# Attention, two MoE layers, one core: another order for the work and the loads of the first two token blocks

## Chip, cores, metric

One core of one Trainium2 chip runs the whole kernel. The metric is the device time of one execution in microseconds (us), as the median of several executions.

## What is computed

The reference, cut to its arithmetic (B = 4 batches, H = 8 heads, S = 576 positions, D = 64; then 2304 tokens of width 512):

```python
def _attn_ref(q, k, v, g_norm):
    kv = np.einsum('bhsd,bhse->bhde', k, v)
    out = np.einsum('bhsd,bhde->bhse', q, kv)
    rms = np.sqrt(np.mean(out * out, axis=-1, keepdims=True) + 1e-06)
    return (out / rms * g_norm)

def _moe_ref(x, w1, w2, w3, w_out):          # w1, w2, w3: 512 x 768, w_out: 768 x 512
    h = np.maximum(np.maximum(x @ w1, x @ w2), x @ w3)
    return (h @ w_out)

def _moe2_ref(x, domain_probs, w1, w2):      # 4 experts, 512 x 1024 and 1024 x 512
    p = domain_probs / (domain_probs.sum(-1, keepdims=True) + 1e-09)
    for e in range(E):
        out += p[:, e:e + 1] * (np.maximum(x @ w1[e], 0.0) @ w2[e])
```

The weights of the first MoE layer arrive as float64. The kernel takes each as a 128 x 512 piece of 64-bit words and makes float32 of it with integer operations.

## The kernel before

The 2304 tokens are worked on in six blocks of 384. The kernel first computes the attention of all tokens, mixed with the first MoE layer for blocks 0 and 1, then the first MoE layer for blocks 2 to 5, then the second MoE layer. Everything is recorded in one hand-made order: each engine runs its instructions in the order in which the program text issues them, and all loads go through the one queue of SyncE (SP in the profile). Matrix products that need precision take each operand as a rounded part ("hi") and a rest ("lo") and add three products.

The change touches the first stretch only, that is attention plus the first MoE layer of blocks 0 and 1. Two strings of tokens set its order.

The string `order` (L634) is the order of the loads. `k` loads one half of a batch's k and v (four DMAs, together 1.18 MB; half 0 serves heads 0 to 3), `q` loads one group of 256 query positions (512 KB; `q2` is the tail group, in four DMAs), `w` loads one weight piece (512 KB). `pump` (L639) issues from the head of this list as far as buffers allow: six for q, three pairs for k and v, three for weight pieces. It is called once at the start and after each step. Behind its first call stand the two small loads of `g_norm` (L660) and the VectorE instruction that doubles `g` (L661).

The string `steps` (L678) is the order of the work. A dot and letters behind a step name the engines of its copies: a is ACT, v is DVE, p is POOL.

- `Kbc` (att_kv): 20 matmuls of 64 columns for two heads of batch b. The fourth of a batch copies the result from the PSUM bank into the tile kvb by four copies.
- `Ti` (att_T): eight transposes of query group i and two copies into the tile qT.
- `Oi` (att_O): 16 matmuls of qT with kvb, two squares on ACT, two sums and one scale-and-add on DVE. `Ni` (att_N): the norm, one ACT and four small DVE operations, then two multiplications on DVE.
- `Xi` (att_X): eight transposes back and two copies into yT. `Sj` (split_x): the hi and lo parts of block j (128 x 1536).
- `Aijf` (moe1_a): product i of block j for the feature group f, 12 matmuls, followed by a copy or a maximum. `Hjf`: hi and lo of the hidden values. `Pf` (moe1_o): block 0 times the w_out piece f, 12 matmuls.
- `a` and `b`: the conversion of weights, by position. Each `a` (conv_a, L217) starts three things for three successive weights: the split into hi and lo of the oldest one (split_h on the engine named first, split_l on POOL where the second letter is p), conv0 of the newest (an ACT operation and a minimum on POOL, L197 and L198), and it leaves conv1 of the middle one (three DVE operations, L205, L206, L209), and a lo part on DVE, for the next `b`.

The converted weights lie in 24 places (w_buf), so none of them is reused in this stretch. PSUM banks are taken in turn: three for transposes and A products, four for O and P, one for K.

Of the kernel before, what the change touches and what calls it, by code (L numbers as in the profile page):

```python
# [21 lines left out]
def tile_attn_moe_moe2(  # L22
# [23 lines left out]
    nc = tc.nc  # L46
# [8 lines left out]
    T = 384  # L55
# [7 lines left out]
    def f32(ap):  # L63
        return ap.bitcast(F32)
# [94 lines left out]
    worder = [("a", 0, 0)]  # L159
    for f in range(NF):  # L160
        worder += [("a", 1, f), ("a", 2, f)] + [("a", 0, f + 1)] * (f + 1 < NF) + [("o", 0, f)]
    N1 = 4 * NF
# [16 lines left out]
    def split_h(w, t, eng="a"):  # L179
        copy(eng, w[:, 0, :], t)  # L180

    def split_l(eng, w, t, key):
        eng.tensor_tensor(out=w[:, 1, :], in0=t, in1=f32(w[:, 0, :]), op=ALU.subtract)  # L183
        wt[key] = w

    def new_w(key):
        return w_buf[worder.index(key)]
# [4 lines left out]
    conv = {}  # L192
# [18 lines left out]
        )  # L211

    cpos = [0, 0, 0, 0]

    def conv_a(pool, eng="ap"):  # L217

        rest = []
        if cpos[3] < cpos[2]:  # L220
            key = worder[cpos[3]]
            w, t = new_w(key), conv.pop(key)
            split_h(w, t, eng[0])
            cpos[3] += 1
            if eng[1] == "p":
                split_l(nc.gpsimd, w, t, key)
            else:
                rest.append(lambda: split_l(nc.vector, w, t, key))
        if cpos[2] < cpos[1]:
            key1 = worder[cpos[2]]  # L230
            rest.insert(0, lambda: conv1(pool, key1))
        if cpos[1] < cpos[0]:
            conv0(pool, worder[cpos[1]])
            cpos[1] += 1
        return rest

    def load_w_to(pool, n):
        while cpos[0] < min(n, N1):
# [379 lines left out]
    with tc.manual_schedule():  # L618
        cv_cm = tc.tile_pool(name="cvp", bufs=3, reuse_waits="tile")
        cvp = cv_cm.__enter__()  # L620
# [9 lines left out]
        for t in kvb:  # L630
# [1 line left out]


        order = (  # L634
            "k00 q0 k01 q1 q2 k10 k11 q3 q4 q6 k20 q5 k21 k30 k31 w w w q8 q9 w"
        ).split()
        free = {"q": 6, "k": 3}

# [28 lines left out]
        def new_acc(n):  # L667
            return [bank("acc") for c in range(n)]
# [7 lines left out]


        steps = (  # L678
# [8 lines left out]
        ).split()  # L687
        for st in steps:
            st, *en = st.split(".")
            kind, at = st[0], [int(x) for x in st[1:]]  # L690
            if kind == "T":
                att_T(xq, *at, *en)
                free["q"] += 1
            elif kind == "K":
                att_kv(kvb, *at, *en)
                free["k"] += at[1] % 2
            elif kind == "O":
                att_O(xq, kvb, *at)
                if at[0] == len(groups) - 1:
                    att_cm.__exit__(None, None, None)  # L700
                    wp = ctx.enter_context(tc.tile_pool(name="wp", bufs=1, side="right", reuse_waits="tile"))
                    wr.append(wp.tile([P, 16 * 2 * DM], F32R, name="wr"))
                    w_buf.extend(part(wr[0], n * 2 * DM, 2 * DM, 2) for n in range(16))
            elif kind == "X":
                att_X(*at, *en)
                if at[0] == len(groups) - 1:
                    xq_cm.__exit__(None, None, None)
                    hs_cm = tc.tile_pool(name="hs", bufs=NF, side="right", reuse_waits="tile")
                    hs = hs_cm.__enter__()
            elif kind == "N":  # L710
                att_N(*at)
            elif kind == "A":
                i, j, f = at
                moe1_a(i, j, f, xs[j], *en)
            elif kind == "H":
                j, f = at
                hidden[j, f] = moe1_split(hs if j else None, j, f, *en)
            elif kind == "P":
                acc = acc or new_acc(KD)
                moe1_o(*at, hidden.pop((0, *at)), acc)  # L720
            elif kind == "S":
                xs.append(split_x(*at, *en))
            elif kind == "a":
                rest = conv_a(cvp, *en)
            elif kind == "b":
                for fn in rest:
                    fn()
            pump()
        assert cpos[3] == N1
        cv_cm.__exit__(None, None, None)  # L730
        moe1_store(0, acc)
        xs = xs[2]
# [54 lines left out]
        for e in range(E):  # L787
            for pr in range(NPR):
                n = (e * NSB - 1) * NPR + pr
# [11 lines left out]
        for n, (e, sb, pr) in enumerate(rounds):  # L801
            last_sb = sb == NSB - 1
            more = not (e == E - 1 and last_sb)
            rest = iter(())
            if before is not None:
                e0, sb0, pr0 = before
                rest = second(n - 1, pr0)
# [60 lines left out]
```

## Time and profile before

| | |
|---|---|
| median of 3 executions | 1148.13 us (1147.34 to 1148.51) |
| the profiled execution | 1146.83 us, its span 1145.0 us |
| PE (TensorE matmul) | 1120.5 us busy, 98% of the span |
| PEld (TensorE weight load) | 1031.7 us |
| DVE (VectorE) | 562.7 us, 49% |
| ACT (ScalarE) | 390.9 us, 34% |
| POOL (GpSimd) | 236.8 us, 21% |
| chain that ended last | PE 88%, DVE 5%, DMA 2%, SPq 2%, ACT 1% |

The page cuts the span into 40 slices of 28.6 us. In tenths (9 is 90% or more), PE's busy share is 6 in the first slice, 9 in the next three, 8 in the fifth, and 9 in all others but the last (8). DVE shows 1, 8, 8, 9, 8, 6 in the first six slices and 2 to 7 later. The DMA row shows 9, 9, 3, 4, 4, 1 in the first six. So the first stretch is where something other than PE can decide. Busy time of an engine that nobody waits for costs nothing; the rows further below are therefore mainly waits and starts.

### The profile page before, as it was taken

Reading aid. Unit: us, or ns where it says so; the run is one execution under the profiler, and the core shown is the slowest. Engines: PE = TensorE matmul, PEld = TensorE weight load, DVE = VectorE, ACT = ScalarE, POOL = GpSimd, SP = SyncE. Lnnn points to the kernel's source line nnn. Section 1 sums busy time; section 2 is a strip of 40 time slices with the busy share of each in tenths; the row PEclk is TensorE's granted clock in tenths of the full one; section 3 lists DMA queues with packets and bytes.
Section 4 is the critical chain, followed back from the end, with each engine's and each line's share of the span. In section 5 each row is a group of like instructions: output and inputs, shape, how many; then the busy total and the mean of one; then the engine's idle time right before and its main releaser. Section 6 shows DMA issues by size and latency. Waiting matters only on the chain.

```text
span 1145.0 us, 15032 instructions
## 1 busy us (share of the span) xinstructions
PE 1120.5 (98%) x6096; PEld 1031.7 (90%) x6096; DVE 562.7 (49%) x842; ACT 390.9 (34%) x699; POOL 236.8 (21%) x178
## 2 busy tenths in 40 slices
PE   6999899999999999999999999999999999999998
PEld 5888899999999888889888988888888888888887
DVE  1889862222325544344754436573535576343523
ACT  3653321121113434253634233452424253332321
POOL 1356740000401320205220202412020522011000
PEclk9999999999999999999999999999999999999999
DMA  9934410000201402014140403332030625040111
GB/s 255 283 107 130 147 47 29 1 28 1 65 29 37 157 1 102 9 56 138 60 171 1 165 1 131 127 122 99 29 138 9 212 65 193 1 153 14 48 63 56
DMA packets 77990, 99.59 MB, mean 87 GB/s; under 512 B 10336, under 2 KB 53344, under 8 KB 77920
## 3 DMA queue, kind: packets, MB, share of 16 engines
q1 hardware_dynamic: 77920, 98.62, 27.0%
q8 instruction: 48, 0.79, 0.3%
q14 instruction: 22, 0.18, 0.0%
HBM read 75.01 MB, written 23.59 MB: 86 GB/s over the span
## 4 chain that ended last, share of the span: by engine, by line
PE 88%; DVE 5%; DMA 2%; SPq 2%; ACT 1%; issue 1%; POOL 1%; DVEq 0%; ACTq 0%
PE bank L575 35%; PE bank L535 30%; PE bank L247 15%; PE bank L413 6%; DMA v<-in_v_dram 1%; DVE cv_a L206 1%; DVE cv_a L209 1%; PE bank L269 1%; DMA k<-in_k_dram 1%; PE bank L362 1%; DVE cv_a L205 1%; SPq L154 0%; PE bank L319 0%; DVE fa L392 0%; SPq L135 0%
## 5 line engine op out<-in xcount | busy, mean ns | idle before, releaser
L575 PE MATMUL bank<-wr,hr 128*128 128x512 f32 x792 | 227.0, 395 | 0.0
L559 DVE TENSOR_TENSOR fa<-bank,fa 128x384 f32<-128x384 f32 x144 | 80.1, 557 | 212.5 <-ACT fa L556 119.2
L575 PEld LDWEIGHTS bank<-wr,hr 128*128 128x128 f32 x792 | 147.0, 188 | 20.7
L517 POOL TENSOR_TENSOR fa<-fa 128x768 f32<-128x768 f32 x48 | 97.3, 2037 | 300.2 <-DMA fa<-y_d 243.0
L247 PE MATMUL bank<-xr,wr 128*128 128x384 f32 x792 | 145.2, 340 | 5.6 <-DVE fa L392 2.2
L247 PEld LDWEIGHTS bank<-xr,wr 128*128 128x128 f32 x792 | 139.6, 188 | 8.4 <-DVE fa L392 3.2
L486 POOL TENSOR_TENSOR w1s<-w1s 128x256 f32<-128x256 f32 x64 | 53.9, 862 | 421.8 <-DMA w1s<-in_moe_w_dram 374.7
L556 ACT ACTIVATE fa<-bank 128x384 f32<-128x384 f32 x144 | 70.6, 490 | 194.3 <-PE bank L535 194.3
L535 PE MATMUL bank<-rb,wr 128*128 128x384 f32 x648 | 131.5, 338 | 0.3 <-DVE hr L543 0.3
L535 PE MATMUL bank<-xr,wr 128*128 128x384 f32 x648 | 131.6, 338 | 0.0
L535 PEld LDWEIGHTS bank<-rb,wr 128*128 128x128 f32 x648 | 116.6, 188 | 10.2 <-DVE hr L543 0.6
L535 PEld LDWEIGHTS bank<-xr,wr 128*128 128x128 f32 x648 | 116.7, 188 | 9.6
L575 PE MATMUL bank<-wr,xr 128*128 128x512 f32 x324 | 100.8, 396 | 0.0
L392 DVE TENSOR_TENSOR fa<-bank,fa 128x384 f32<-128x384 f32 x72 | 39.8, 555 | 117.7 <-PE bank L247 117.5
L247 PE MATMUL bank<-xr,wl 128*128 128x384 f32 x504 | 90.5, 335 | 0.0
L247 PEld LDWEIGHTS bank<-xr,wl 128*128 128x128 f32 x504 | 87.4, 188 | 0.2 <-DVE wl L183 0.2
L575 PE MATMUL bank<-wl,hr 128*128 128x512 f32 x288 | 86.3, 394 | 0.0
L543 DVE SCALAR_TENSOR_TENSOR hr<-fa,hr 128x384 fp32r<-128x384 f32 x72 | 50.0, 695 | 42.6 <-ACT hr L542 42.6
L575 PEld LDWEIGHTS bank<-wr,xr 128*128 128x128 f32 x324 | 60.7, 188 | 10.8
L542 ACT ACTIVATE hr<-fa 128x384 fp32r<-128x384 f32 x72 | 37.8, 525 | 77.4 <-DVE fa L559 77.4
L575 PEld LDWEIGHTS bank<-wl,hr 128*128 128x128 f32 x288 | 53.4, 188 | 6.9
L542 ACT ACTIVATE xr<-fa 128x384 fp32r<-128x384 f32 x48 | 25.2, 525 | 96.7 <-DVE fa L559 96.7
(132 smaller groups left out, 1477.5 us busy)
## 6 DMA issues: line engine op xcount, KB each, us to landing
fa<-y_d SPq DMA_DIRECT2D x22, 768.0 KB, 6.2
stage_a<-in_moe_w_dram SPq DMA_DIRECT2D x18, 512.0 KB, 3.4
o_d<-fa SPq DMA_DIRECT2D x36, 256.0 KB, 3.7
fa<-o_d SPq DMA_DIRECT2D x36, 256.0 KB, 5.3
w1s<-in_moe_w_dram SPq DMA_DIRECT2D x32, 256.0 KB, 3.1
w2s<-in_moe_w_dram SPq DMA_DIRECT2D x32, 256.0 KB, 4.0
y_d<-fa SPq DMA_DIRECT2D x6, 768.0 KB, 3.8
o_d<-ob SPq DMA_DIRECT2D x18, 256.0 KB, 2.0
```

What stands on the lines that cost most here:

```text
L205: nc.vector.tensor_scalar(out=ti, in0=ti, scalar1=3, scalar2=None, op0=ALU.logical_shift_left)
L247: nc.tensor.matmul(ps, w[:, wi, c * P : (c + 1) * P], x[xi][:, c, :], start=(n == 0), stop=(n == 3 * KD - 1),)
L392: nc.vector.tensor_tensor(out=ms[j, f], in0=ps[:, :T], in1=ms[j, f], op=ALU.max)
L413: nc.tensor.matmul(acc[c][:, :T], w[:, wi, c * P : (c + 1) * P], h[hi], start=(f == 0 and n == 0), stop=(f == NF - 1 and n == 2),)
L486: eng.tensor_tensor(out=st[:, o], in0=st[:, a], in1=st[:, b], op=ALU.subtract)
L517: eng.tensor_tensor(out=yb[:, o], in0=yb[:, a], in1=yb[:, b], op=op)
L535: nc.tensor.matmul(out, w[wi][:, c * P : (c + 1) * P], y[yi][:, c, :], start=(i == 0 and k in BEGIN), stop=(i == 5), skip_group_check=k no ...
L542: nc.scalar.activation(out=h[0], in_=src, func=AF.Relu)
L543: nc.vector.scalar_tensor_tensor(out=h[1], in0=src, scalar=0.0, in1=f32(h[0]), op0=ALU.max, op1=ALU.subtract)
L556: nc.scalar.activation(out=s[k // 2], in_=a, func=AF.Copy)
L559: nc.vector.tensor_tensor(out=t, in0=x, in1=t, op=ALU.add)
L575: nc.tensor.matmul(banks[i], h[a, i // TPB][hi][:, i % TPB * P : (i % TPB + 1) * P], w[a][wi], start=(pr == 0 and a == 0 and m == 0), stop ...
```

## The change

The helper that converted by position is gone. Each stage of each weight is now a step of its own: `cN` is conv0 of weight N, `dN` conv1, `sN` its split with the engines named behind the dot. The two strings are new. No arithmetic is added or removed; the last two stretches of the program are as before.

```diff
-    cpos = [0, 0, 0, 0]
-    def conv_a(pool, eng="ap"):
...
+    cpos = [0, 0, 0]
+    def conv2(key, eng="ap"):
+        w, t = new_w(key), conv.pop(key)
+        split_h(w, t, eng[0])
+        split_l(nc.gpsimd if eng[1] == "p" else nc.vector, w, t, key)
...
-            "k00 q0 k01 q1 q2 k10 k11 q3 q4 q6 k20 q5 k21 k30 k31 w w w q8 q9 w"
+            "q1 q0 k00 k01 w q2 k10 k11 q3 w q4 k20 k21 q6 q5 k30 k31 w w q8 q9"
...
-            "K00 T0 K01 K02 K03 T1 O0 O1 K10 a N0 T2.av b K11 a N1 K12 K13 T3.av O2 b X0 N2 O3 T4 X1 "
-            "a.vp b O4 N3 K20 T5 a b a.vv K21 K22 N4 K23 X2 S0.pp X3 S1.vp O5 T6 b N5 K30 X4.va a.pp O6 "
-            "K31 b a.av X5 b K32 K33 N6 T8 a O7 b T9 O8 A000 a X6 b N7 A010 a.vp b A100 a.vp O9 b X7 "
...
+            "K00 K01 T1.av T0 K02 K03.avav c0 O1 O0 N1 K10 N0 T2 K11 d0 X1 K12 K13.vvaa T3.av X0.vv O3 T4.va "
+            "N3 c1 O2 K20 s0.pp O4 K21 N2 X3 K22 N4 T6 K23 d1 S0.pp X2 T5.av O6 S1.pp O5 N6 N5 X4 K30 K31 c2 "
+            "K32 c3 K33 d2 d3 s1.pp s2.pp A000 T8 X6 O8 O7 A200 s3.pp N8 c4 c5 A010 T9 d4 d5 X5 O9 A110 A100 "
...
```

Three places show how the instructions move. The first is the head of DVE's queue. Before, behind the doubling of g stand the sums of O0 and O1 (ss) and the first norm (rr); kvb_124 below is the tile of batch 0, bank_73 the bank of the K steps.

```order
L661 TENSOR_SCALAR g_75<-g_75 128x1
L333 TENSOR_REDUCE ss_253<-xt_244 128x8 x2
L334 TENSOR_SCALAR a_254<-ss_253 128x16
L333 TENSOR_REDUCE ss_269<-xt_260 128x8 x2
L334 TENSOR_SCALAR a_270<-ss_269 128x16
```

The same place of DVE's queue in the changed kernel:

```order
L645 TENSOR_SCALAR g_75<-g_75 128x1
L70 COPY qT_192<-bank_71 128x512
L70 COPY kvb_124<-bank_73 64x4x64 x2
L317 TENSOR_REDUCE ss_256<-xt_247 128x8 x2
L318 TENSOR_SCALAR a_257<-ss_256 128x16
```

One copy of T1 (qT_192) and two of K03 (kvb_124), which were ACT's, now stand on DVE between the doubling of g and the first sums.

The second place is the head of the queue of loads on SP. Before:

```order
L153 DMA k_0_128<-in_k_dram 128x4x256
L154 DMA k_0_128<-in_k_dram 64x4x64
L153 DMA v_0_131<-in_v_dram 128x4x256
L154 DMA v_0_131<-in_v_dram 64x4x64
L139 DMA q_134<-in_q_dram 128x8x128
```

And in the changed kernel, from its first load to the g load (the k01 pair and the rest of k10 left out):

```order
L139 DMA q_128<-in_q_dram 128x8x128
L139 DMA q_130<-in_q_dram 128x8x128
L153 DMA k_0_132<-in_k_dram 128x4x256
L154 DMA k_0_132<-in_k_dram 64x4x64
L153 DMA v_0_135<-in_v_dram 128x4x256
L154 DMA v_0_135<-in_v_dram 64x4x64
...
L176 DMA stage_a_0_144<-in_moe_w_dram 128x4x128
L135 DMA q_146<-in_q_dram 32x8x128 x4
L153 DMA k_0_151<-in_k_dram 128x4x256
...
L644 DMA g_75<-in_g_norm_dram 64x1 x2
```

Two query groups now stand ahead of the first k and v, and a weight piece (stage_a) ahead of the g load.

The third place is DVE's queue around the step T5, whose tile is qT_478 before and qT_583 after. Before, both its copies are on ACT, behind a norm's square root:

```order
L342 ACTIVATE s_459<-ss_415,eps 128x16
L68 ACTIVATE qT_478<-bank_72 128x512
L68 ACTIVATE qT_478<-bank_70 128x512
L342 ACTIVATE s_525<-ss_452,eps 128x16
L68 ACTIVATE kvb_124<-bank_73 64x4x64 x4
```

In the changed kernel this is DVE's queue from the end of N2 over N4 and d1 (cv_a) to T5's second copy:

```order
L337 TENSOR_TENSOR xt_443<-bank_68,rr_510 128x512
L327 RECIPROCAL rr_538<-s_537 128x16
L328 TENSOR_TENSOR rr_538<-a_479,rr_538 128x16
L329 TENSOR_TENSOR rr_538<-rr_538,s_537 128x16
L330 RECIPROCAL rr_538<-rr_538 128x16
L337 TENSOR_TENSOR xt_469<-bank_69,rr_538 128x4x2x64
L337 TENSOR_TENSOR xt_469<-bank_66,rr_538 128x4x2x64
L205 TENSOR_SCALAR cv_a_0_440<-cv_a_0_440 128x512
L206 SCALAR_TENSOR_TENSOR cv_a_0_440<-stage_a_0_188,cv_a_0_440 128x512
L209 SCALAR_TENSOR_TENSOR cv_a_0_440<-stage_a_0_188,cv_a_0_440 128x512
L70 COPY qT_583<-bank_72 128x512
```

T5's second copy now stands on DVE behind a norm and a conversion.

## Rows read from the trace of the kernel before

**Rows 1.** Stretches: busy PE, PEld, DVE, ACT, POOL; clock; DMA share; GB/s
```profile
0.00:57.80 57.80, 45.80 (x532) 40.91 (x532) 28.37 (x63) 28.69 (x57) 15.09 (x15) 0.97 1.10 269
57.80:100.00 42.20, 40.50 (x266) 38.75 (x265) 38.58 (x71) 22.13 (x43) 25.53 (x18) 1.00 0.34 110
100.00:128.00 28.00, 23.06 (x123) 20.82 (x122) 27.28 (x38) 9.27 (x17) 20.51 (x15) 1.00 0.44 138
128.00:165.70 37.70, 37.67 (x213) 37.34 (x213) 30.13 (x45) 11.53 (x20) 24.64 (x20) 1.00 0.23 77
165.70:1145.00 979.30, 973.43 (x4970) 893.84 (x4968) 438.33 (x629) 319.29 (x564) 151.02 (x112) 1.00 0.22 74
```

**Rows 2.** Groups by line, PE, 57.9 to 128 us: busy, mean | idle before
```profile
L247 PE MATMUL bank<-xr,wr 128*128 128x384 f32 x101 | 19.7, 346 | 4.9 <-DVE fa L392 1.6 <-ACT fa L68 1.5 <-ACT wr L68 1.0
...
L295 PE MATMUL bank<-ident,q 128*128 128x128 f32 x16 | 2.2, 278 | 1.2 <-DMA q<-in_q_dram 1.2
```

**Rows 3.** Timeline of PE, start: start us, us, what [idle before]
```profile
7.56 1.53 PE L269 MATMUL bank<-v,k 128*64 128x64 f32 x20 [7.56 <-DMA v<-in_v_dram]
9.59 1.94 PE L295 MATMUL bank<-ident,q 128*128 128x128 f32 x8 [0.49 <-DMA q<-in_q_dram]
...
18.09 4.97 PE L319 MATMUL bank<-kvb,qT 128*128 128x128 f32 x32
```

**Rows 4.** Rate of the DMA engines, 5 to 56 us
```profile
DMA packets 21486, 14.32 MB, mean 281 GB/s; under 512 B 4687, under 2 KB 21481, under 8 KB 21481
```

**Rows 5.** The load of g (timeline of SP; its tile) and DVE's first instruction
```profile
16.57 1.19 SPq L660 DMA_DIRECT2D g<-in_g_norm_dram  x2
...
DMA to landing us min/median/max: 6.2/6.4/6.5
...
23.78 0.15 DVE L661 TENSOR_SCALAR g<-g 128x1 f32<-128x1 f32 x1 [23.78 <-ACT xt L332]
```

**Rows 6.** Timeline of ACT and DVE: the copies of kvb and qT
```profile
16.52 1.56 ACT L68 ACTIVATE kvb<-bank 64x256 f32<-64x256 f32 x4 [4.36 <-PE bank L269]
...
28.89 0.68 DVE L70 COPY qT<-bank 128x512 f32<-128x512 f32 x1
```

**Rows 7.** Timeline of PE, 42 to 58 us: a wait, then steps at full clock
```profile
42.94 1.88 PE L269 MATMUL bank<-v,k 128*64 128x64 f32 x40 [1.81 <-DMA v<-in_v_dram]
...
49.45 1.04 PE L295 MATMUL bank<-ident,q 128*128 128x128 f32 x8
50.41 0.95 PE L269 MATMUL bank<-v,k 128*64 128x64 f32 x20
...
52.22 1.95 PE L319 MATMUL bank<-kvb,qT 128*128 128x128 f32 x16
54.10 0.95 PE L269 MATMUL bank<-v,k 128*64 128x64 f32 x20
54.98 1.09 PE L362 MATMUL bank<-ident,xt 128*128 128x128 f32 x8
56.00 1.82 PE L269 MATMUL bank<-v,k 128*64 128x64 f32 x40
```

**Rows 8.** Stretches around the changes of PE's pace, columns as in Rows 1
```profile
18.20:20.60 2.40, 2.40 (x13) 2.40 (x13) 0.00 (x0) 1.54 (x3) 1.04 (x1) 1.00 1.12 290
21.00:23.00 2.00, 2.00 (x20) 1.88 (x18) 0.00 (x0) 1.20 (x2) 0.00 (x0) 1.00 1.14 283
44.60:47.90 3.30, 3.30 (x19) 3.18 (x18) 1.90 (x6) 2.97 (x7) 0.00 (x0) 0.50 1.16 267
```

**Rows 9.** Timeline of POOL and DVE during the lo parts of S0 and S1
```profile
38.53 3.44 POOL L376 TENSOR_TENSOR xr<-fa,xr 128x1536 fp32r<-128x1536 f32 x1
48.78 3.46 POOL L376 TENSOR_TENSOR xr<-fa,xr 128x1536 fp32r<-128x1536 f32 x1 [6.81 <-DVE xr L70]
...
39.73 2.27 DVE L334 TENSOR_SCALAR a<-ss 128x16 f32<-128x16 f32 x1
```

**Rows 10.** Groups by line, DVE, first 196 us: busy, mean ns of conv1's second
```profile
L206 DVE SCALAR_TENSOR_TENSOR cv_a<-stage_a,cv_a 128x512 int32<-128x512 int32 x18 | 18.2, 1012 | 0.6
```

More of the change, by code (lines that the diff above doesn't have):

```diff
@@ L211, in conv1 @@
         )
-    cpos = [0, 0, 0, 0]
-    def conv_a(pool, eng="ap"):
[L219 to L235, printed above, removed]
+    cpos = [0, 0, 0]
[3 more added lines that the diff above has]
+        split_l(nc.gpsimd if eng[1] == "p" else nc.vector, w, t, key)
     def load_w_to(pool, n):
@@ L689, in tile_attn_moe_moe2 @@
             st, *en = st.split(".")
-            kind, at = st[0], [int(x) for x in st[1:]]
-            if kind == "T":
+            kind = st[0]
+            at = [int(st[1:])] if kind in "cds" else [int(x) for x in st[1:]]
+            if kind in "cds":
+                n = at[0]
+                if kind == "c":
+                    conv0(cvp, worder[n])
+                elif kind == "d":
+                    conv1(cvp, worder[n])
+                else:
+                    conv2(worder[n], *en)
+            elif kind == "T":
                 att_T(xq, *at, *en)
@@ L722, in tile_attn_moe_moe2 @@
                 xs.append(split_x(*at, *en))
[L723 to L727, printed above, removed]
             pump()
-        assert cpos[3] == N1
+        assert cpos[2] == N1
         cv_cm.__exit__(None, None, None)
```

11 rows, old and new, of the table steps are left out of this document.

## Prediction

> **What bounds the kernel now.** I read the table of stretches first [rows 1]. From 165.7 us on, where the changed strings end, PE is busy 973.4 of 979.3 us, and the change touches nothing there: that part can only be shifted. So the question is when PE ends the first stretch (165.7 us before). In it PE is idle 12.0 us up to 57.8, 1.7 from there to 100 and 4.9 from 100 to 128, 18.7 in all with the last part. Each of these has another cause. Up to 57.8 us the DMA engines run without a gap at 281 GB/s [rows 4], and PE waits for k, v and q. From 100 to 128 DVE is busy 27.3 of 28.0 us [rows 1] while PE waits 4.9 us for maxima, copies and splits [rows 2]; with T8's wait for q8 (1.2 us) and 0.5 of small waits it is 6.6 us behind K33. K33 is the last step of the last batch's k and v; it starts with K32 at 56.00 and both take 1.82 us [rows 7], so it ends at 57.8. I use that point as a hinge: how much later or earlier does the new order reach it, and what of the 6.6 us behind it goes away.
>
> **The start: loads.** Two q groups of 512 KB (524,288 bytes) now stand ahead of the first k and v. At 281 GB/s each takes 1.87 us, so K00 starts at 7.56 + 3.7 = 11.3 us [rows 3]. Then PE has enough to do: K00, K01, T1, T0, K02, K03 at the slow pace of the start, 1.53 for a K and 1.94 for a T, are 10.0 us, and PE is through at 21.3. Up to there nothing is lost that the loads would not cost anyway.
>
> **The start: DVE's first instruction.** The next step, O1, needs all of K03's copies and T1's. Two of the former and one of the latter now stand on DVE, in its queue behind the doubling of g. That instruction ran at 23.78 us [rows 5]: its two loads were issued from 16.57 on in 1.19 us and the later one took 6.5 us to land, which is 23.7. The row names ACT as the releaser, but its time is that of the landing, and the operation reads g. Before, this cost nothing, since DVE's next work, O0's sums, came at the same time. Now the g load has one weight piece more ahead of it (1.87 us): it lands at about 25.5. Behind it come 0.15 us, the copy of qT (0.68 us) and three copies of kvb in turn, DVE, ACT, DVE; ACT's took 1.56/4 = 0.39 each [rows 6], DVE's, of half a qT copy's columns, lie between that and 0.68, and I take 0.4. O1 starts at 25.5 + 0.15 + 0.6 + 1.2 = 27.4 us, after 6 us of idle PE. It ran at 18.09 before [rows 3].
>
> The Trainium skill, "TensorE: Matmul & The Clock Gate", section "Architectural detail: the array is 16× 32×32, not 1× 128×128", says that VectorE's queue is strictly first in, first out. No row of before shows a ready instruction behind a waiting one on DVE, so the trace does not test it; without that rule O1 would start near 22.5, which is the fast rival's case.
>
> **From O1 to K33's end** PE has 12 K, 5 T, 6 full O, the half O2, 4 X and the half X2 to do. By the distance of starts in the rows at full clock [rows 7] they take 0.90, 0.96, 1.88, 1.0 (X): 10.8 + 4.8 + 11.3 + 1.6 + 4.0 + 0.5 = 33.0 us. Loads no longer limit this: up to k31 there are 14.16 MB (8 pairs of 1.18 MB, 7 q, 2 weight pieces), 50.4 us at 281 GB/s, so the last k and v are there at about 55. Without any other wait K33 ends at 27.4 + 33.0 = 60.4. Two costs come on top.
>
> *Clock.* Where PE's pace is half, the rows show it: 13 matmuls in 2.40 us from 18.2, of the same step as 20 in 2.00 us from 21.0, and a granted clock of 0.50 (1.2 GHz) from 44.6 to 47.9 [rows 8]. The half level at 44.6 came after PE had waited 1.81 us for the k and v of K22, to 42.94 [rows 7]. A gap of 6 us should bring it too. One such stretch of 3.3 us costs 1.7 us; the ends are 0 and two stretches, 3.3. I take 1.7. The skill's same page, "Part 1: The HAM clock gate", says that the default is the throttled state and that activity releases it; the first part agrees with [rows 8], and how soon it is released behind the gap no row of before settles.
>
> *DVE behind POOL.* While POOL ran S0's lo part (38.53 + 3.44 = 41.97), a small DVE operation (128 x 16) took 2.27 and ended at 42.00 [rows 9]; S1's lo part takes as long. Such DVE operations on SBUF are thus held to the end of POOL's long two-input one. Before, nobody on PE waited for them. Now T5's second copy stands on DVE behind N2, N4 and d1 (about three times 1.0 us [rows 10]), and O5 needs it for its second half; O5 also needs N4's bank and X2 needs N2. Both lo parts, 6.9 us of POOL, fall into these 10 us of DVE work, because S1 starts when X2 and X3 are copied. Without a block the copy is just in time. With one block PE waits 2 to 4 us, with both up to 5.6; none is possible if the small operations fall between. I take 3.0, near the single block.
>
> So K33 ends at 60.4 + 1.7 + 3.0 = 65.1 us. Before, the same work ended at 57.8 - 1.0 = 56.8, since X5 (1.0) has moved behind K33 and must be taken off. **The first part loses 8.3 us** (3.6 to 12.5 at the bounds).
>
> **Behind K33.** The PE work is the same, plus X5, already counted. Before, one conv1 was done by then, now two; the moves of splits and copies to POOL and ACT take off DVE one conv1 (2.5 us), one X copy (0.7), three weight splits (1.8) and a little more, 5.2 us in all against the 4.9 us that PE waited for in the stretch where DVE was full. POOL gets 3.8 us more; it was busy 46 of 70 us from 57.8 to 128 [rows 1], so it has room. The q8 wait (1.2) goes too, since PE is late and the load is not. Of the 6.6 us I leave 1.2 for maxima that wait behind a conversion: **the second part gains 5.4 us** (bounds 3.5 and 6.6).
>
> **Sum.** 8.3 - 5.4 = +2.9 us, against the profiled execution 1146.83 + 2.9 = 1149.7. The median lies 1.30 above the profiled one, so 1148.13 + 2.9 = 1151.0 us.
>
> **Rivals.** About 0.2% (2.3 us) is what a measurement of this kernel can tell from no change.
>
> *Fast: g does not hold O1*, because DVE lets copies pass or g lands early. O1 starts at 22.5; 33.0 us of work and 1 us of slow clock would end at 56.5, and k31's landing puts K33's end at 57.5 or later. That is +0.7, and with the gain of 5.4 the time is 1143.4. For it: PE has earlier weights and never waits for a load again. Against it: the order itself, and that g's landing and DVE's first start agree to 0.1 us. Chance 0.14.
>
> *Same: g holds, nothing else does.* The blocks of POOL miss DVE's work, so 60.4 + 1.7 = 62.1, +5.3, and the 5.4 behind K33 come back: 1148.0. It decides at T5's copy: if that ends before O5's first half does, this is the case. For it: that copy reads PSUM, and a holding hits it only through what stands ahead of it. Chance 0.31.
>
> *Forecast: g holds O1 and a block holds O5*, 1151.0 as summed. Chance 0.40.
>
> *Worse: both blocks and two slow stretches*, or POOL, with six splits more, becomes the late one behind K33: 60.4 + 3.3 + 5.6 = 69.3, +12.5, with 3.5 given back: +9.0, 1157.1. Chance 0.15.
>
> **How the numbers follow.** Faster by over 0.2% (below 1145.8): the fast rival and a little of the second, 0.17. Within: most of the second and the low end of the forecast (1148.8 to 1150.4), 0.29. Slower: 0.54. The likeliest case alone spans 1148.8 to 1154. The range leaves out most of the fast and a part of the worse case: 1144.5 to 1156.
>
> **What would show it.** Right, if DVE's first row stands at 25 to 26 us with g, PE is idle before O1 to about 27, K32 is waited for by no load, and a small DVE row in front of O5 lasts until POOL's split ends. Behind K33 the waits for DVE should be 1 to 3 us instead of 5. Wrong, if O1 starts before 24, if K33 ends before 60, or if PE waits again 5 us between 100 and 130.

## The result, and the profile after

The changed kernel takes 1159.95 us (median of 4 executions, 1158.78 to 1160.95); the kernel before, on the same chip, 1147.74 us. The ratio is 1.0109, 95% interval 1.0091 to 1.0126: about 12 us slower. The direction was as forecast, the size was not: 1159.95 lies above the range's upper end of 1156.

The profiled execution took 1160.95 us, its span is 1159.1 us, 14.1 more than before. Cut at the same places of the program as [rows 1], the table of stretches (columns as there) reads:

```profile
0.00:73.90 73.90, 45.65 (x524) 40.53 (x524) 39.84 (x78) 25.83 (x51) 20.34 (x20) 0.91 0.88 228
73.90:100.00 26.10, 25.14 (x183) 24.20 (x180) 24.43 (x40) 16.98 (x34) 19.41 (x16) 1.00 0.32 101
100.00:130.00 30.00, 29.01 (x168) 28.43 (x167) 28.87 (x39) 9.24 (x17) 23.45 (x19) 1.00 0.34 108
130.00:179.50 49.50, 47.08 (x261) 45.28 (x260) 46.69 (x61) 11.08 (x20) 40.10 (x28) 1.00 0.28 84
179.50:1159.10 979.60, 973.59 (x4970) 894.27 (x4969) 435.88 (x629) 319.46 (x564) 152.77 (x112) 1.00 0.22 74
```

The last line is the last one of [rows 1] within 0.3 us: the rest of the program was only shifted. All of the loss lies in the first line. K33 ends at 73.9 and not at 57.8 us, and PE is idle for 28.2 us of that stretch (73.90 - 45.65), where it had been idle for 12.0.

The timeline of PE in this stretch, of its lines those that begin with a long wait or mark a place (start us, us, what, idle before and its releaser):

```profile
10.65 3.00 PE L253 MATMUL bank<-v,k 128*64 128x64 f32 x40 [10.65 <-DMA v<-in_v_dram]
...
16.80 1.82 PE L253 MATMUL bank<-v,k 128*64 128x64 f32 x40
26.33 5.80 PE L303 MATMUL bank<-kvb,qT 128*128 128x128 f32 x32 [7.71 <-DVE kvb L70]
...
42.31 0.66 PE L346 MATMUL bank<-ident,xt 128*128 128x128 f32 x4 [2.22 <-ACT qT L68]
...
58.49 0.63 PE L346 MATMUL bank<-ident,xt 128*128 128x128 f32 x4 [2.71 <-DVE xt L337]
...
66.86 1.49 PE L303 MATMUL bank<-kvb,qT 128*128 128x128 f32 x8 [4.20 <-DVE qT L70]
...
70.00 4.00 PE L253 MATMUL bank<-v,k 128*64 128x64 f32 x80
```

In order these are K00, K02 with K03, O1 with O0, the second half of X0, the second half of X2, the second half of O5, and K30 to K33. Before, O1 began at 18.09 [rows 3], and no wait of this stretch behind O1 was longer than the 1.81 us at 42.94 [rows 7]. Now there are four, and every one of them leads to DVE's queue, X0's by way of ACT. Here is DVE's timeline around the first, third and fourth:

```profile
25.08 0.15 DVE L645 TENSOR_SCALAR g<-g 128x1 f32<-128x1 f32 x1 [25.08 <-DMA g<-in_g_norm_dram]
25.15 0.68 DVE L70 COPY qT<-bank 128x512 f32<-128x512 f32 x1
25.86 0.42 DVE L70 COPY kvb<-bank 64x256 f32<-64x256 f32 x1
26.72 0.43 DVE L70 COPY kvb<-bank 64x256 f32<-64x256 f32 x1 [0.45 <-ACT kvb L68]
...
53.73 3.37 DVE L328 TENSOR_TENSOR rr<-a,rr 128x8 f32<-128x8 f32 x1
...
61.69 3.80 DVE L206 SCALAR_TENSOR_TENSOR cv_a<-stage_a,cv_a 128x512 int32<-128x512 int32 x1
...
66.13 0.68 DVE L70 COPY qT<-bank 128x512 f32<-128x512 f32 x1
```

and the timeline of POOL, the lo parts of S0 and S1:

```profile
53.64 3.43 POOL L360 TENSOR_TENSOR xr<-fa,xr 128x1536 fp32r<-128x1536 f32 x1
...
61.45 3.48 POOL L360 TENSOR_TENSOR xr<-fa,xr 128x1536 fp32r<-128x1536 f32 x1
```

DVE does nothing for its first 25.08 us: the doubling of g stands at the head of its queue, and the copies that O1 needs stand behind it. The copy of qT had been ready since about 15.8 us (a run below shows it). Later a product of 128 x 8 numbers takes 3.37 us and ends at 57.10, 0.03 after POOL's S0 lo part (57.07); X2 waits for it. L206, otherwise 0.69 us, takes 3.80 and ends 0.6 after the S1 lo part; O5's copy of qT stands behind it.

The wait in front of X0's second half has the same form, without POOL. DVE again:

```profile
38.12 0.42 DVE L205 TENSOR_SCALAR cv_a<-cv_a 128x512 int32<-128x512 int32 x1
38.58 0.69 DVE L206 SCALAR_TENSOR_TENSOR cv_a<-stage_a,cv_a 128x512 int32<-128x512 int32 x1
39.30 0.69 DVE L209 SCALAR_TENSOR_TENSOR cv_a<-stage_a,cv_a 128x512 int32<-128x512 int32 x1
39.91 0.84 DVE L70 COPY kvb<-bank 64x256 f32<-64x256 f32 x2
```

The step d0 (1.8 us) stands ahead of DVE's two copies of K13. ACT's two copies of K13 come after them, then ACT's copy of T3, which frees the bank that X0 wants.

The clock, in stretches laid around its changes:

```profile
23.80:30.60 6.80, 4.19 (x20) 3.90 (x21) 2.28 (x5) 1.75 (x4) 2.48 (x2) 0.54 1.16 299
...
44.30:47.60 3.30, 3.30 (x23) 3.06 (x23) 1.93 (x4) 1.16 (x3) 0.00 (x0) 0.58 1.13 296
...
68.20:71.50 3.30, 3.30 (x35) 2.81 (x35) 2.82 (x10) 2.54 (x6) 0.00 (x0) 0.58 0.31 122
```

The granted clock is near its lower level, 1.2 GHz, in three stretches (0.54, 0.58, 0.58), behind three of the four gaps. Before there was one such stretch behind O1 [rows 8].

Behind K33 the groups of PE (74 to 180 us; busy, mean | idle before) show what is left of [rows 2]:

```profile
L231 PE MATMUL bank<-xr,wr 128*128 128x384 f32 x264 | 48.3, 340 | 1.2 <-DVE fa L376 1.0 <-DVE wr L70 0.2
...
L397 PE MATMUL bank<-hr,wr 128*128 128x384 f32 x60 | 11.7, 342 | 1.2 <-DVE hr L70 1.2
```

With 1.0 us each at X7 and at the first P product these are 4.4 us of waits, where there had been 6.6.

### The profile page after: what moved, and what is told of

It reads as the page before. It is cut to its first block, busy times and chain, and to the rows that moved or that the text cites. A ratio compares the mean times of both kernels' runs of the same rounds, so it can differ in the third digit from the quotient of the medians.

```text
span 1159.1 us, 15049 instructions
## 1 busy us (share of the span) xinstructions
PE 1120.5 (97%) x6096; PEld 1032.7 (89%) x6096; DVE 575.7 (50%) x843; ACT 382.6 (33%) x683; POOL 256.1 (22%) x193
## 4 chain that ended last, share of the span: by engine, by line
PE 89%; DVE 6%; issue 2%; DMA 1%; SPq 1%; ACT 1%; POOL 0%; DVEq 0%; ACTq 0%; POOLq 0%
PE bank L559 35%; PE bank L519 30%; PE bank L231 16%; PE bank L397 6%; DVE cv_a L206 1%; PE bank L303 1%; DVE cv_a L205 1%; DMA g<-in_g_norm_dram 1%; DMA q<-in_q_dram 1%; DVE xt L337 1%; DVE rr L328 1%; DVE fa L376 1%; PE bank L346 0%; DVE cv_a L209 0%; PE bank L253 0%
## 5 line engine op out<-in xcount | busy, mean ns | idle before, releaser
L397 PE MATMUL bank<-hr,wr 128*128 128x384 f32 x300 | 57.4, 339 | 1.2 <-DVE hr L70 1.2
```

The source lines that it names most:

```text
L397: nc.tensor.matmul(acc[c][:, :T], w[:, wi, c * P : (c + 1) * P], h[hi], start=(f == 0 and n == 0), stop=(f == NF - 1 and n == 2),)
```

## Experiments

**Theory A**: the loss is the holds in VectorE's queue, that is copies which TensorE needs and which stand behind something that can't start (g) or can't finish (operations beside POOL's lo parts, d0), plus the slow clock behind the gaps. **Rival B**: it is the new order of loads, which brings k and v later. **Rival C**: conversions on VectorE or POOL are the bound behind K33, so what is gained ahead of K33 is given back.

Runs are compared by their ratio to the kernel before on the same chip; beside these runs that kernel took 1147.74 to 1149.26 us, so a difference between two medians of the table is uncertain by up to 1.5 us for that reason alone. The last two columns are from the profiled execution: the end of K33, and the time from there to the end of the span. For the kernel before and e3, X5 is taken off the former and put into the latter (1.0 us), so that the work is the same.

| kernel | median us | ratio, 95% interval | K33 ends | rest |
|---|---|---|---|---|
| before | 1147.74 | 1 | 56.8 | 1088.2 |
| changed | 1159.95 | 1.0109 (1.0091 to 1.0126) | 74.0 | 1085.1 |
| e1 g later | 1151.8 | 1.0024 (1.0013 to 1.0034) | 64.3 | 1085.3 |
| e2 lo parts cut in four | 1155.68 | 1.0055 (1.0040 to 1.0070) | 69.6 | 1083.9 |
| e10 d0 behind X0 | 1159.42 | 1.0095 (1.0081 to 1.0108) | 72.6 | 1084.9 |
| e4 these three together | 1147.11 | 0.9985 (0.9975 to 0.9994) | 63.3 | 1084.3 |
| e6 changed, O5 freed | 1157.34 | 1.0074 (1.0060 to 1.0087) | 67.3 | 1087.7 |
| e5 e4 with O5 freed | 1145.76 | 0.9970 (0.9958 to 0.9982) | 58.7 | 1085.8 |
| e12 e5 with d1 earlier | 1145.71 | 0.9980 (0.9971 to 0.9988) | 58.2 | 1087.0 |
| e7 changed, k00 first | 1162.19 | 1.0119 (1.0105 to 1.0133) | 76.3 | 1084.5 |
| e8 e5, k00 first | 1145.99 | 0.9976 (0.9967 to 0.9985) | 57.2 | 1086.2 |
| e11 load of g first | 1154.92 | 1.0056 (1.0041 to 1.0072) | 67.2 | 1084.5 |
| e9 6 extra products | 1160.17 | 1.0101 (1.0088 to 1.0115) | 73.6 | 1084.6 |
| e13 26 extra products | 1158.36 | 1.0085 (1.0061 to 1.0110) | 71.5 | 1085.3 |
| e3 old steps, new loads | 1156.42 | 1.0060 (1.0045 to 1.0075) | 64.9 | 1089.9 |

**e1: the doubling of g behind N0**

```diff
-        nc.vector.tensor_scalar(out=g2, in0=g2, scalar1=2.0, scalar2=None, op0=ALU.mult)
...
-            "... K03.avav c0 O1 O0 N1 K10 N0 T2 K11 d0 ..."
+            "... K03.avav c0 O1 O0 N1 K10 N0 g T2 K11 d0 ..."
...
```

> The changed kernel with one instruction moved: the doubling of g stands on VectorE behind the norm N0 instead of at the head of its queue. Theory A (three holds in VectorE's queue cost the time: g before O1, d0 before kvb's copies, POOL's split in front of X2 and O5): O1 starts near 20.5 us instead of 26.3, the half clock behind the gap (6.8 us) goes as well, and the time falls by 5 to 9 us, to 1151 to 1155. Rival B (the new order of the loads makes PE late): O1 is earlier, but PE then waits for k, v and q, and the time falls by at most 2 us. Rival C (the conversions behind the attention are the bound, whatever the start costs): the gain comes back as waits for VectorE behind K33, time within 2 us of 1160.

Measured: 1151.8 us, ratio 1.0024. The head of DVE's queue and its new place of the doubling:

```profile
15.82 0.69 DVE L70 COPY qT<-bank 128x512 f32<-128x512 f32 x1 [15.82 <-PE bank L279]
19.13 0.42 DVE L70 COPY kvb<-bank 64x256 f32<-64x256 f32 x1 [2.62 <-ACT kvb L68]
...
30.09 0.14 DVE L677 TENSOR_SCALAR g<-g 128x1 f32<-128x1 f32 x1
```

The same copy of qT now runs at 15.82 and not at 25.15, and O1 starts at 19.60. This one instruction in that place cost some 8 to 10 us, two thirds or more of the whole loss (1.0109 - 1.0024 = 0.0085 of 1148 us is 9.8; the medians differ by 8.2). In the trace K33 ends 9.7 us earlier. O1 and O0 also run at full clock in this execution (4.50 us from O1's start to O0's end, against 5.80), which is 1.3 us of the gain; in e4, e5 and e12, with the same move, the half level is there (last section), so that part does not come with the move each time.

**e2: the lo parts of S0 and S1 in four pieces on POOL**

```diff
...
+            for c in range(KD):
+                nc.gpsimd.tensor_tensor(
+                    out=xs[1][:, c, :], in0=yT[j][:, c, :], in1=f32(xs[0])[:, c, :], op=ALU.subtract
+                )
...
```

> The changed kernel with the lo part of S0 and S1 on POOL cut into four operations of 128 x 384 instead of one of 128 x 1536. Theory A: a VectorE operation is held only to the end of one piece (about 0.9 us), the rows of 3.4 and 3.8 us become 1 to 1.5, PE's waits at X2 and O5 (2.7 and 4.2 us) shrink to under 2 together, and the time falls by 4 to 7 us, to 1153 to 1156. Rival B: no change beyond 1 us, since PE would wait for loads. If VectorE is held by POOL's whole work and not by one instruction, the waits stay: 1160.

Measured: 1155.68 us, ratio 1.0055, in the expected range. DVE's rows there:

```profile
52.44 0.93 DVE L328 TENSOR_TENSOR rr<-a,rr 128x8 f32<-128x8 f32 x1
53.41 0.92 DVE L329 TENSOR_TENSOR rr<-rr,s 128x8 f32<-128x8 f32 x1
...
59.22 1.37 DVE L206 SCALAR_TENSOR_TENSOR cv_a<-stage_a,cv_a 128x512 int32<-128x512 int32 x1
60.63 1.37 DVE L209 SCALAR_TENSOR_TENSOR cv_a<-stage_a,cv_a 128x512 int32<-128x512 int32 x1
```

The same L328 is held for 0.93 and not 3.37 us, and X2's wait falls from 2.71 to 0.45 us. So the length of POOL's instruction sets the hold. But each further instruction is held by the next piece: two of d1's three take 1.37 where they take 0.69 alone, so that O5's wait falls only from 4.20 to 2.96. Together the two waits are 3.4 us, where under 2 had been expected.

**e10: d0 behind X0**

```diff
-            "... K11 d0 X1 K12 K13.vvaa T3.av X0.vv O3 ..."
+            "... K11 X1 K12 K13.vvaa T3.av X0.vv d0 O3 ..."
```

> The changed kernel with the step d0 behind X0 and nothing else, so that d0's three VectorE operations no longer stand ahead of K13's copies of kvb. Theory A by the stalls: X0's wait of 2.2 us falls to about 0.8, and if the half level from 44.3 us goes with it another 1.7 comes back: 1157 to 1159. By what the first runs left for it (8.1 us for g, 4.3 for the uncut lo parts, 12.8 for all three together) only 0.4 remains: 1159 to 1160. Rival (VectorE's work merely changes places): 1160.

Measured: 1159.42 us, ratio 1.0095: the second of the expected ranges. X0's wait fell from 2.22 to 1.06 us, but O4's two halves then waited 0.28 and 0.97 us that they hadn't in the changed kernel's trace, X2 still 1.92 and O5 4.19. (Of the 0.97, about 0.47 stands in the traces of e2, e6 and e7 too, where d0 was not moved.) d0's work is partly only moved from one wait to another; what it cost is 0.5 us by the medians and 1.6 by the ratios, within the measurement's uncertainty.

**e4: the three together**

```diff
-            "... N1 K10 N0 T2 K11 d0 X1 K12 K13.vvaa T3.av X0.vv O3 ..."
+            "... N1 K10 N0 g T2 K11 X1 K12 K13.vvaa T3.av X0.vv d0 O3 ..."
```

(with e1's and e2's other lines)

> The changed kernel with the doubling of g behind N0, the lo parts of S0 and S1 in four pieces, and the conversion d0 moved behind X0. Theory A: PE's waits of 7.7, 2.2, 2.7 and 4.2 us go for the most part, and the half clock behind them; PE is then at the pace of the loads, K33 ends near 58 to 62 us instead of 73.9, and the time is 1144 to 1150, at or below before. Rival B: 1157 to 1160. Rival C: K33 early, but 5 us and more of new waits behind it, time over 1152.

Measured: 1147.11 us, ratio 0.9985, in the middle of A's range. The load order is the changed one. So the time of before comes back with all loads in their new order, by changes in VectorE's queue and in the POOL work that holds it. It does not come back in the same place: K33 still ends 6.5 us later than before (63.3 against 56.8, where 58 to 62 had been expected), O5 still waits 3.16 us, and 3.9 us are gained behind K33. The single gains by the medians, 8.2 + 4.3 + 0.5 = 13.0, are close to the 12.8 of all three; by the ratios they are 0.0153 against 0.0124. Within the intervals both fit, so that the three add up is likely and not shown.

**e3: the old steps with the new loads** (only the string of loads replaced in the kernel before)

> The kernel before with the new order of the loads alone. Theory A: K00 starts at 10.6 instead of 7.6 us, but PE had waits of 4 us for loads behind that, of which some fill up; the sums behind O0 start with g at 25 instead of 23.8; time 1147 to 1150, no more than 2 us over before. Rival B: the loads are the cost, and the time is 1155 to 1160.

Measured: 1156.42 us, ratio 1.0060, a miss for theory A's number (1147 to 1150) and inside rival B's (1155 to 1160). The traces of PE and of POOL tell why:

```profile
10.60 1.53 PE L269 MATMUL bank<-v,k 128*64 128x64 f32 x20 [10.60 <-DMA v<-in_v_dram]
...
27.77 1.97 PE L295 MATMUL bank<-ident,qr 128*128 128x128 f32 x8 [2.92 <-POOL qr L290]
...
51.99 2.05 PE L362 MATMUL bank<-ident,xt 128*128 128x128 f32 x8 [2.41 <-DVE xt L353]
```
```profile
25.24 1.49 POOL L198 TENSOR_SCALAR cv_a<-cv_a 128x512 f32<-128x512 f32 x1 [21.92 <-ACT cv_a L197]
26.68 1.04 POOL L290 COPY qr<-q 128x1024 f32<-128x1024 f32 x1
```

K00 starts 3.0 us later than before, but no k or v is waited for behind it. The old steps convert weights by position, so the early weight of the new loads turned the first `a` into real work: a minimum on POOL ahead of the copy qr that T2 needs, and later conversions on DVE ahead of a norm that X2 needs, of which one operation (L344, 0.17 us alone) is held to 1.22 beside POOL. The run thus doesn't test the loads alone; it shows once more that the cost of a piece of work is what stands behind it in its queue. Against B it says only that behind K00 late k and v are not what PE waits for. What weighs against B is e4: the same loads, and no loss.

**e5 and e6: O5 freed** (T5's copies both on ACT, d1 behind O5; e5 on top of e4, e6 alone on the changed kernel)

```diff
-            "... T6 K23 d1 S0.pp X2 T5.av O6 S1.pp O5 N6 ..."
+            "... T6 K23 S0.pp X2 T5 O6 S1.pp O5 d1 N6 ..."
```

> As the kernel with the three holds taken away (1147.1), and T5's second copy on ACT with d1 moved behind O5. In that kernel O5 still waited 3.2 us, since each of d1's three operations was held by one of POOL's four pieces, and a stretch of half clock (3.4 us, worth 1.7) followed. Theory A: both go, time falls by 3 to 5 us, to 1142 to 1144.5. Rival C (VectorE's sum of work behind K33 is the bound): d1 is only done later, the gain comes back behind K33, and the time stays at 1146 to 1148.

> The changed kernel with only T5's second copy on ACT and d1 behind O5; g and POOL's split stay as they are. Theory A (the holds add up, each is paid by PE): the wait of 4.2 us at O5 goes, and about 1 us of the half clock behind it; the others stay; time falls by 4 to 6 us, to 1154 to 1156. If the holds overlap, so that g's wait alone sets the end: 1159 to 1160.

Measured: e5 1145.76 us, ratio 0.9970, faster than the changed kernel and the one before; e6 1157.34 us, ratio 1.0074. By the medians they gain 1.4 and 2.6 us, by the ratios 1.7 and 4.0; 3 to 5 and 4 to 6 had been expected, so e5 is below its range and e6 at the low end or below. O5's wait is gone in both, and K33 ends 4.6 and 6.7 us earlier. But the rest behind K33 takes 1.5 and 2.6 us longer (so the profiled spans differ by 3.1 and 4.1). Two rows of PE in e5 behind K33 that e4 did not have:

```profile
66.35 0.97 PE L231 MATMUL bank<-xr,wl 128*128 128x384 f32 x4 [0.71 <-POOL wl L70]
68.02 3.77 PE L231 MATMUL bank<-xr,wl 128*128 128x384 f32 x20 [0.71 <-POOL wl L183]
```

In e6 the same two waits are 1.25 and 0.70 us. Both are for one weight, the third (A200): four products with its hi part, then the rest with its lo part, which POOL splits one after the other as soon as DVE has ended d2 (65.49 us in e5). d2 stands behind N6 and N5, and these now stand behind d1: it ends 6.8 us behind K33 in e5 and 7.3 in e6, against 4.6 in e4 and 3.8 in the changed kernel. So rival C holds in part: conversions are late again behind K33, and a third or more of what is gained ahead of it is given back. Since d1 was moved in every kernel that shows this, it isn't shown how much of it is d1's new place and how much the earlier K33.

**e12: d1 into a gap of VectorE in e5**

```diff
-            "... S0.pp X2 T5 O6 S1.pp O5 d1 N6 ..."
+            "... S0.pp X2 T5 d1 O6 S1.pp O5 N6 ..."
```

> The kernel with no hold at O5 (1145.8), with d1 moved from behind O5 to behind T5, where VectorE stood idle for 0.9 us. If the two waits of 0.7 us in front of the first products of block 0 with their second and third weights come from conversions that VectorE takes up too late, both fall: 1144.4 to 1145.2. If POOL is the limit there (rival C), nothing moves: 1145.8.

Measured: 1145.71 us, ratio 0.9980, no gain over e5. PE and DVE:

```profile
63.14 1.14 PE L346 MATMUL bank<-ident,xt 128*128 128x128 f32 x8 [1.78 <-ACT fa L68]
```
```profile
51.28 1.34 DVE L205 TENSOR_SCALAR cv_a<-cv_a 128x512 int32<-128x512 int32 x1
52.66 1.37 DVE L206 SCALAR_TENSOR_TENSOR cv_a<-stage_a,cv_a 128x512 int32<-128x512 int32 x1
54.06 1.38 DVE L209 SCALAR_TENSOR_TENSOR cv_a<-stage_a,cv_a 128x512 int32<-128x512 int32 x1
```

The first of the two waits fell from 0.71 to 0.29 us, the second stayed at 0.70, and a new one of 1.78 came ahead of them. The second is POOL's: the lo part takes it 1.59 us, the four products with the hi part 0.97. The first fell though d2 ended later (66.53), because PE had been held by the new wait. The gap that had been free beside POOL's pieces was not free for d1: its three operations are again held, to 1.34 to 1.38 us each, and the sums and norms behind them, and ACT's work behind these, came later.

**e7 and e8: k00 ahead of the two q** (e7 on the changed kernel, e8 on e5)

```diff
-            "q1 q0 k00 k01 w q2 ..."
+            "k00 q1 q0 k01 w q2 ..."
```

> The changed kernel with k00 ahead of the two q loads. Theory A: K00 starts at 7.6 instead of 10.6 us, but O1 waits for g as before, and the time stays within 1.5 us of 1160. Rival B (late loads at the start are part of the cost): the time falls by 3 us or more.

> The kernel without holds at O1, X0, X2 and O5, with k00 loaded ahead of the two q groups. Theory A: without the hold at O1 the start of K00 counts, unless PE then waits for k10 and k11 at their old times; gain against the same kernel with q first 0 to 3 us, time 1140 to 1144. Rival B: 3 us and more.

Measured: e7 1162.19 us, ratio 1.0119; e8 1145.99 us, ratio 0.9976. K00 starts at 7.99 and 7.78 us instead of 10.65 and 10.87, and neither kernel gains from it. e7 is 2.2 us above the changed kernel by the medians, a little more than the 1.5 allowed for, and 1.1 by the ratios. In e7 the load of g was issued later, and DVE's first row is

```profile
28.08 0.15 DVE L645 TENSOR_SCALAR g<-g 128x1 f32<-128x1 f32 x1 [28.08 <-DMA g<-in_g_norm_dram]
```

3.0 us later than in the changed kernel. O1 starts 3.0 us later (29.34), and K33 ends 2.3 us later. PE's early work had begun 2.7 us sooner; the end followed g and not the k and v. B's form of the loss, that K00's late start costs, falls. The new steps with the old loads were not run, so what the later landing of g (25.1 us against 23.8) costs by itself isn't measured.

**e11: the load of g ahead of all others** (the doubling stays at the head of DVE's queue)

```diff
-        pump()
         for h in range(2):
             nc.sync.dma_start(out=g2[h * D : (h + 1) * D, :], ...)
+        pump()
```

> The changed kernel with the two loads of g issued ahead of all others; the doubling stays where it is in VectorE's queue. Theory A (it is the landing of g that holds the queue's head): O1 starts at 20 to 21 us, about as with the doubling moved, later by the 1.2 us that the two issues take: 1151 to 1154. Rival B (load order is what costs, and g's delay is only one sign of it): no more than 1 us better than 1160, since all other loads are 1.2 us later.

Measured: 1154.92 us, ratio 1.0056, 0.9 above A's range and 4 below B's bound. PE's start:

```profile
13.87 2.99 PE L253 MATMUL bank<-v,k 128*64 128x64 f32 x40 [13.87 <-DMA v<-in_v_dram]
...
22.54 0.49 PE L303 MATMUL bank<-kvb,qT 128*128 128x128 f32 x2 [0.99 <-DVE kvb L70]
```

and SP's first row:

```profile
2.24 1.23 SPq L643 DMA_DIRECT2D g<-in_g_norm_dram  x2
```

The hold is gone without any move in DVE's queue, so it is g's landing that mattered. K00 starts 3.2 us later, though the two issues take only 1.2; O1 follows 2.9 us later than in e1, and the time is 3.1 us above e1's. Most of the rest is a second hold of the same kind, on SP: the load of g waits 1.6 us for an ACT operation that also writes g (L612, 2.01 to 2.21 us), and all other loads now stand behind it. The first q is issued at 3.51 us instead of 0.71, and the first k at 4.76 instead of 1.83, 2.9 us later.

**e9 and e13: PE kept busy ahead of O1**

```diff
-            "... K03.avav c0 O1 O0 ..."
+            "... K03.avav c0 f0 O1 O0 ..."
...
+            elif kind == "f":
+                for n in range(26):
+                    nc.tensor.matmul(banks[3][:, 0:P], ident, ident, start=True, stop=True)
```

(e13; e9 had f60 and range(at[0]), which is 6)

> The changed kernel with 60 products of the identity with itself put between K03 and O1, into a bank that O0 overwrites: TensorE works through most of the 7.7 us in which it waited there, and nothing else moves. They are work that the result doesn't need. Theory A, its part on the clock (the half level from 23.8 to 30.6 us of the changed kernel follows from the gap): O1 starts where it did, at 26.3 us, O1 and O0 take about 3.8 us instead of 5.8, and the time falls by about 2, to 1157 to 1158.5. If the slow pace behind the gap comes from something else, 1160 as the changed kernel. If the 60 products outlast the gap, O1 starts later and the time rises by as much.

> The changed kernel with 26 products of the identity with itself between K03 and O1, into a bank that O0 overwrites; they are work that the result doesn't need. In the run before (e9_pe_kept_busy) the step's number was read digit by digit, so that 6 products ran and not 60: they took 1.6 us, PE still waited 6.2 us, and the half level stayed. By that pace 26 take 6.9 of the 7.8 us from K03's end to O1. Clock follows the gap: the half level from 23.8 to 30.6 us is gone, O1 starts at 26.3 us as it did, O1 and O0 take about 3.8 us instead of 5.8, and the time is 1157 to 1158.5. Clock comes from something else: O1 and O0 take 5.8 us as before and the time is 1160.

Measured: e9 1160.17 us, where 6 products left a wait of 6.2 us and the half level stayed, so it decides nothing. e13 1158.36 us, ratio 1.0085. PE's rows, and two stretches:

```profile
18.69 6.07 PE L687 MATMUL bank<-ident 128*128 128x128 f32 x52
26.88 0.49 PE L303 MATMUL bank<-kvb,qT 128*128 128x128 f32 x2 [2.12 <-DVE kvb L70]
27.75 3.62 PE L303 MATMUL bank<-kvb,qT 128*128 128x128 f32 x30 [0.39 <-DVE kvb L70]
```
```profile
44.30:47.60 3.30, 3.30 (x50) 2.90 (x47) 2.92 (x9) 2.18 (x5) 1.25 (x1) 1.00 1.06 287
57.50:60.50 3.00, 3.00 (x16) 3.00 (x15) 2.96 (x4) 1.06 (x2) 2.88 (x2) 0.50 1.15 322
```

With the gap filled O1 and O0 run at full pace: from 27.75 their last 30 rows take 3.62 us, where 32 took 5.80. That fits a low clock that follows the idle time. One trace doesn't show it, since e4, e5, e8 and e12 have the half level at O1 behind short waits (last section). What it was worth is less than the pace alone says: O1 started 0.55 us later since g landed later (25.62), and the half stretch at 44.3 was gone as well, but another came at 57.5. K33 ends 2.5 us earlier than in the changed kernel; the medians differ by 1.6 us, by intervals that overlap. The stretch at 57.5 also shows that the two costs don't simply add: it makes O6 1.6 us longer (4.40 against 2.84 for its 24 rows), and the wait behind it, for O5's copy, 1.6 shorter (2.59 against 4.20).

## Why the prediction was right or wrong

**Start of K00 (11.3 forecast, 10.65 measured) and K03's end (21.3, measured 18.6).** The first is right. PE was through earlier because its pace rose earlier than in the kernel before: K02 and K03 take 0.91 us each at 16.80, against 1.5 before at 13.41. Why it rose is not shown. It changed nothing, since O1 could not start.

**O1 (27.4 forecast, 26.33 measured).** The mechanism is right but for its last link: DVE's first instruction at 25.08 with g's landing (25.5 forecast), then the copy of qT (0.68) and three copies of kvb in turn on DVE, ACT and DVE. But O1 did not wait for all three: it started 0.05 us behind the end of the first (26.28), while the others ran from 26.31 and 26.72. I had summed all three (1.2 us); this is 0.8 of the 1.1 by which O1 came earlier, and g's landing the rest. e1 (doubling moved), e11 (load moved) and e7 (landing 3.0 later, O1 3.0 later) show this cause apart from all others. The page "TensorE: Matmul & The Clock Gate" of the Trainium skill, section "Architectural detail: the array is 16× 32×32, not 1× 128×128", which has VectorE's queue as strict first in, first out, is confirmed: with the doubling moved, the copy that was held to 25.15 ran at 15.82.

**The work from O1 to K33 (33.0).** Right. In e5 this stretch takes 38.15 us (20.55 to 58.70), with 3.3 us of waits in the rows and one stretch of half clock (about 3.4 us, worth 1.7); 33.1 to 33.2 remain.

**Clock (1.7 forecast, about 4.9 measured).** Wrong in size. From O1 to K33's end it takes 74.0 - 26.3 = 47.7 us; less 33.0 of work and 9.7 of waits, 4.9 remain. From the stretches: PE worked at half level for 4.3 us from 26.33, and for 3.3 twice, 10.9 in all, half of which is 5.4. I had counted one stretch and bounded at two; there were three, behind three of the four gaps. e13 doesn't measure it by itself: from O1 to K33's end it takes 3.0 us less (44.7 against 47.7), but its waits there are 1.3 us shorter too (8.4 against 9.7), so 1.7 are left for the clock.

**DVE held (3.0 forecast, bounds 0 to 5.6; 9.7 measured).** This is the step that failed most. I wrote "With one block PE waits 2 to 4 us, with both up to 5.6" and took one. Both lo parts fell on DVE work that PE waited for: X2 waited 2.71 and O5 4.20 us, 6.9 together, as long as the two lo parts themselves and more than my bound. The remaining 2.8 are X0's 2.22 and X1's 0.59, waits that the sum put at nothing: I had let K33 end at 60.4 "without any other wait", and had not followed d0 past K13's copies in DVE's queue, as I had followed T5's. e2 shows the POOL part (X2's wait falls to 0.45, O5's to 2.96) and e6 that O5's goes with d1 and T5's copy; e10 shows that d0 was the cause of about half of X0's wait. X1's stands in e10 as well (0.59); by its row it waits for the product of N1 on DVE, and no run tested it.

**K33's end (65.1 forecast, 74.0 measured).** -1.1 at O1, +6.7 of waits, +3.2 of clock make 8.8 of the 8.9 us; as the clock's 4.9 is itself a remainder, this sum doesn't test it. The first part lost 17.2 us (57.8 - 1.0 to 74.0), beyond the bound of 12.5.

**Behind K33 (5.4 us gained forecast, 3.1 measured).** Right in sign, too large. The rest of the span is 1088.2 before and 1085.1 after; 2.2 us of it are waits of the rows (6.6 against 4.4), the rest none that they name. I had left 1.2 us of waits. In no run of the table is the gain above 4.3, and in e6 it is 0.5. It is smaller, 0.5 to 2.4, in the four kernels in which d1 stands later (e5, e6, e8, e12), and 2.9 to 4.3 in the others with the new steps, whose K33 ends anywhere from 63 to 76 us. So the place of d1 goes with it, and by these runs the lateness of K33 alone does not.

**The sum and the rivals.** +17.2 - 3.1 is +14.1 in the profiled executions, 12.2 in the medians, against +2.9. The step that failed is thus the 3.0 us for DVE's holds (9.7), and next to it the clock (1.7, about 4.9); the hold of g, the largest single cost, was forecast. Fast and Same fell at O1 and O5. Worse (1157.1) had the right picture, both blocks and more than one slow stretch, with 0.15; against it X0's and X1's waits (2.8), the third slow stretch (1.6) and the longer blocks (1.3) were missing, less the 1.1 at O1. I gave one block more weight although I had noted that both lo parts lie within the 10 us of DVE work.

Of the marks that I had set, DVE's first row, PE's idle time before O1, the absence of a load wait at K32 and the long DVE row in front of O5 all appeared. The waits behind K33 came out at 4.4 us and not at 1 to 3.

What stays open: how the clock's three stretches divide up among the gaps, since filling one gap also moved the other stretches.

## What to carry to other kernels

When an order is laid out anew, walk each in-order queue from its head and ask of every instruction that a busy engine waits for what stands ahead of it and when that can start; one tiny operation on a load that lands late, at the head of VectorE's queue, cost more here than all else together (8 to 10 us of 12 to 13). Where VectorE has short two-operand work that TensorE waits for, count the whole length of any POOL operation beside it, for each such place and not once for all; shorter POOL pieces bound a single hold, but not a row of them. And allow for a stretch of slow clock behind a gap of TensorE, as a range and not as a sure cost; then ask what the late engine will take back where the gap is closed.

## What the runs showed of the hardware

**A hold lasts as long as POOL's instruction, and is paid anew for each.** In the changed kernel L328 took 0.17 us at 36.14, on 128 x 16 numbers, and 3.37 at 53.73, on half as many, beside a POOL instruction of 3.43. With pieces of about 1 us (3.87 for four) it took 0.93, but d1's three operations, 1.8 us alone, took 4.1 in e12. The page "SBUF — State Buffer" of the Trainium skill, section "Who interferes with whom", says that a VectorE instruction with two SBUF inputs contends with a GpSimd instruction that reads SBUF, that the port pair they share is an exclusive lock, and that the order of issue decides who blocks. The rows of L328 and L206 agree: each started 0.1 to 0.2 us behind POOL's and ended 0.03 and 0.6 us behind its end. By this rule, as by the row of 2.27 us in [rows 9], the price of a hold could have been read off as up to the full lo part.

**The half clock doesn't follow each gap alike.** In the changed kernel X0's wait of 2.22 us was followed by a granted clock of 0.58 from 44.3 and X2's 2.71 by none; in e13 X0's wait was the same 2.22 and the clock stayed at 1.00, but X2's of 2.15 was followed by 0.50 from 57.5. At O1 six kernels waited 6.2 to 11.3 us (the changed one, e2, e6, e7, e9, e10), and all six ran O1 and O0 at the half level (5.6 to 6.9 us). Seven waited 2.1 us or less there: three ran at full pace (e1, e11, e13, the last 30 rows in 3.62 us) and four did not (e4 and e5 5.24, e12 5.07, e8 6.17 for all 32), with 0.50 granted from 21.6 us in e5 behind waits of only 0.99 and 0.39. So a long gap brought the half level each time, a short one sometimes; what decides in the second case these runs don't show.

**A small load takes what stands ahead of it.** The two loads of g (64 values each) have landed after

```profile
DMA to landing us min/median/max: 7.1/7.2/7.4
```

in the changed kernel, where bulk loads are under way, and after

```profile
DMA to landing us min/median/max: 2.3/2.3/2.3
```

in e11, where they are issued first.
